# Feed-forward matmuls as lowest-priority filler, half-size attention units in one segment, and LayerNorm scaling shared with a second engine, in a scheduled two-layer kernel

## The chip, the cores and the metric

The kernel runs on one core of one Trainium2 chip. The metric is device time in microseconds (us) of one execution of the whole program. The kernel before was run three times for the first record: 559.99 us median, 558.21 to 562.43. Every experiment below was timed in turn with the kernel before on the same chip.

A core has several engines that each work through their own instruction list in order. The profile calls them PE (TensorE matmuls), PEld (its weight loads, which overlap PE), DVE (VectorE), ACT (ScalarE), POOL (GpSimd) and SP (SyncE, which here issues the DMA transposes).

## The reference

Two equal layers are applied to x of shape 1 x 2048 x 512 in bf16. Cut to what matters:

```python
x = A_x
for layer in (0, 1):
    x = x + A(layernorm(x), wq, wk, wv, wo, beta)   # attention with a memory
    x = x + B(layernorm(x), w1, w3, w2)             # (silu(x@w1) * (x@w3)) @ w2, 512 -> 1376 -> 512

def A(x, ...):                    # 32 heads of 16, four segments of 512 tokens
    M, z = 0, 0
    for s in range(4):
        a_dot = softmax(qs @ ks.T * scale + causal_mask) @ vs
        a_mem = (phi(qs) @ M) / (phi(qs) @ z + 1e-6)       # phi(t) = t+1 if t>0 else exp(t)
        outs.append(g * a_mem + (1 - g) * a_dot)           # g = sigmoid(beta)
        M, z = M + phi(ks).T @ vs, z + sum(phi(ks))        # carried to the next segment
    return concat(outs) @ wo
```

Three dependences matter. A segment needs the memory of the segment before. Layer 1 of a segment needs layer 0's feed-forward result of the same tokens, that is of the same segment. And the value product needs the masked exponentials.

## The kernel before

A Python program builds a list of operations, each with its dependences, buffers, a priority (the smaller number goes first) and an estimated cost. A list scheduler then fixes, before anything runs, the order of every engine's instructions. On the chip each engine follows its list and waits on semaphores. If an estimate is wrong, the order stays as it was, and the engine waits.

Eight attention segments (g = 0 to 7, four in each layer) each go through: LayerNorm (LN), projections q, k, v, the memory read and update, 20 attention units, the output projection, LN again, and the feed-forward network (FFN). The code below is from the kernel; "..." marks cuts.

```python
# cost of one operation on an engine: (engine, time it occupies the engine, time to its result), in ns
def o_act(n, psum=True):
    return ("act", 114.0 + 0.833 * n, (190.0 if psum else 225.0) + 0.833 * n)
def o_dve(n, psum=False, mode=1.0):
    c = n / 0.96 / mode
    return ("dve", c + (75.0 if psum else 45.0), c + (150.0 if psum else 65.0))
def o_pool(n, per=1.04):
    return ("pool", 170.0 + per * n, 170.0 + per * n)
...
mkpool("S", 1)        # one logit buffer of four PSUM banks
mkpool("B", 4)        # four single banks for everything else
e_r = ring("e", 6, [P, 4, 512])       # six buffers of exponentials
xf_r = ring("xf", 1, [P, NCG, 512])   # one buffer of normalised FFN input
...
# the scale 0.5 of the tanh form of silu is put into w2, on POOL
for a in range(2):
    pool(lambda e, a=a: e.tensor_scalar(w2_sb[:, 5 * a:5 * a + 5, :], w2_sb[:, 5 * a:5 * a + 5, :], 0.5, None, op0=ALU.mult),
         2560, ..., prio=0.9)
...
# LayerNorm: after bn_stats, bn_aggr (DVE) and the power -1/2 (POOL), 128 tokens at a time
dve(lambda e, ...: e.tensor_scalar(xn_r[xn.slot][:], x_tok[:, tt, :], mean, rstd,
        op0=ALU.subtract, op1=ALU.mult), 512, mode=1.3, ..., prio=prio, name="norm")
dmaT(...)                                         # transposed by a DMA
...
# attention unit: logits on PE, exp on ACT, causal mask of the 128 diagonal columns on POOL
u = pe(lg, N / 2.4 + 20, mode="R", ...)           # HP priority: first of all
act(... e.activation(e_r[...][:, :, 0:N], S4[:, :, 0:N], ACT.Exp, scale=SCALE), 4 * N, ...)
pool(... e.affine_select(e_r[...][:, :, c:c + 128], ...), 512, ..., name="mask")
...
pe(av, 1280 / 2.4 + 40, mode="C", reads=[... masked exponentials ...], ...)   # value product, after 3 or 5 units
...
# priorities of PE's other work, by segment g
#   projections        g - 0.95 + 0.05 * n        memory matmuls   g + 0.1 to g + 0.42
#   output projection  g + 0.9                    FFN              from g + 1.35 on
```

PE executes in order. If a value product stands at the head of PE's list and its mask is late, all matmuls behind it wait.

The softmax here doesn't subtract the row's maximum and nothing guards it: scores larger than these inputs give would overflow.

## Time and profile before

| | before |
|---|---|
| time, median of 3 | 559.99 us |
| profiled execution | 560.7 us span |
| PE / DVE / ACT / POOL busy | 86% / 79% / 71% / 42% |

The page's first two parts give each engine's busy time over the span, and the span in 40 slices of 14 us. A digit is the busy share of a slice in tenths; in the PEclk row it is the granted clock of the TensorE.

```profile
PE 484.8 (86%) x3836; PEld 198.4 (35%) x3904; DVE 445.5 (79%) x893; ACT 395.5 (71%) x324; POOL 235.2 (42%) x326
...
PE   1837568758999899999989999999999999989897
...
PEclk9956789877999899999999999999999999999999
```

PE is nearly full from slice 11 on. In the first ten slices it has holes, and its clock is low there. Some PE records are missing (3836 matmuls against 3904 weight loads), so PE's busy time before is a little understated.

The groups of instructions give line, engine, operation, tiles and shapes, count, busy us and mean ns, and then the idle time of the engine before them with what ended it.

```profile
L682 ACT ACTIVATE e<-psall 128x2048 bf16<-128x2048 f32 x160 | 300.3, 1877 | 57.5 <-PE psall L674 55.1
...
L700 PE MATMUL psall<-e,va 128*32 128x512 bf16 (+3 forms) x1024 | 49.2, 316 | 6.2 <-POOL e L685 5.4
...
L515 DVE TENSOR_SCALAR xn<-x_tok,ln 128x512 bf16<-128x512 bf16 x64 | 43.6, 713 | 12.2 <-POOL ln L509 7.6
```

The 160 exps set the beat: 1.877 us each. The 64 LN scalings on DVE take 713 ns on average. The busy time by stage, cut at the first exp, the first exps of segments 1 and 2, and the last exp, comes from the windows view. Its columns are the stretch and its length, then busy us (and instructions) of PE, PEld, DVE, ACT and POOL, the granted clock, the DMA share and GB/s.

```profile
20.50:95.00 74.50, 46.81 (x392) 18.04 (x397) 63.10 (x111) 47.00 (x34) 41.84 (x44) 0.75 0.46 125
95.00:153.30 58.30, 44.85 (x389) 16.52 (x394) 43.73 (x96) 47.09 (x37) 26.44 (x37) 0.82 0.31 55
153.30:481.70 328.40, 314.20 (x2670) 128.34 (x2718) 281.01 (x573) 282.61 (x224) 148.97 (x222) 0.99 0.26 50
481.70:560.70 79.00, 70.79 (x358) 32.69 (x363) 50.78 (x92) 13.76 (x24) 4.58 (x6) 1.00 0.17 42
```

Segment 0 (first row) takes 74.5 us, at a granted clock of 0.75. Segments 2 to 7 (third row) take 54.7 us each, with PE almost always busy at full clock. After the last exp comes a tail of 79 us of FFN and output matmuls.

Two causes of segment 0's length can be read directly. First, the chain of waits (start, us, what) shows the memory matmuls behind a DMA transpose:

```profile
30.92 8.29 DMA pkt<-pk
39.21 0.05 issue
39.26 1.09 PE psall L594 x8
40.34 0.57 PE psall L674 x4
```

PE reaches these memory matmuls before their transpose has landed, and the logits behind them (L674) wait too. Second, the timelines of POOL and then of DVE in the same stretch (start, us, engine, operation):

```profile
49.90 6.68 POOL L485 TENSOR_SCALAR w<-w 128x2560 bf16<-128x2560 bf16 x1
...
58.42 6.66 POOL L485 TENSOR_SCALAR w<-w 128x2560 bf16<-128x2560 bf16 x1
```

```profile
50.44 6.93 DVE L515 TENSOR_SCALAR xn<-x_tok,ln 128x512 bf16<-128x512 bf16 x2
57.29 1.27 DVE L441 CAST va<-psall 128x512 bf16<-128x512 f32 x2
58.48 6.74 DVE L515 TENSOR_SCALAR xn<-x_tok,ln 128x512 bf16<-128x512 bf16 x1
```

While POOL scales w2 for 6.7 us, an LN scaling that otherwise takes 0.4 to 0.7 us on DVE lasts as long as POOL's instruction. The evictions queued behind it on DVE wait.

### The profile page before, as it was taken

The page shows a single profiled execution, that of the slowest core. Times are in us where ns is not written, and L with a number is a line of the kernel's source. Part 1 is how long each engine was busy: PE and PEld are TensorE (multiplying, and loading weights), DVE is VectorE, ACT ScalarE, POOL GpSimd, SP SyncE. Part 2 cuts the span into 40 slices and gives each one's busy share as a digit, 9 for nine tenths or more (in the row PEclk, how much of TensorE's full clock was granted, in tenths as well). Part 3 has the DMA queues.
Part 4 walks back from the last instruction along what each step waited for, and adds up shares of the span by engine and source line. Part 5 has one row for each costly group of instructions (what it writes and reads, how often), then busy time and mean ns, then how long its engine had stood idle before and what let it go on. Part 6 is the DMA issues. An engine that isn't in the chain of part 4 may idle for free.

```text
span 560.7 us, 9831 instructions
## 1 busy us (share of the span) xinstructions
PE 484.8 (86%) x3836; PEld 198.4 (35%) x3904; DVE 445.5 (79%) x893; ACT 395.5 (71%) x324; POOL 235.2 (42%) x326
## 2 busy tenths in 40 slices
PE   1837568758999899999989999999999999989897
PEld 0212123222333333333333433443334433434343
DVE  4558999885769787898877989899987897868573
ACT  1736387877987799889878898888998798322130
POOL 7528843453435435545434544444454444210000
PEclk9956789877999899999999999999999999999999
DMA  5793112324211431143223231323113110220301
GB/s 169 243 275 75 39 39 47 49 49 94 39 29 30 67 67 29 29 85 58 47 39 67 49 67 39 67 48 67 39 39 85 48 40 19 67 66 1 76 0 39
DMA packets 106255, 35.31 MB, mean 63 GB/s; under 512 B 100736, under 2 KB 104832, under 8 KB 106208
## 3 DMA queue, kind: packets, MB, share of 16 engines
q1 hardware_dynamic: 102976, 26.76, 24.1%
q0 software_dynamic: 1504, 6.32, 3.2%
q10 hardware_dynamic: 1728, 1.58, 0.9%
q8 instruction: 31, 0.51, 0.4%
q14 instruction: 16, 0.13, 0.1%
HBM read 8.43 MB, written 2.10 MB: 19 GB/s over the span
## 4 chain that ended last, share of the span: by engine, by line
PE 48%; DVE 24%; DMA 11%; issue 7%; ACT 4%; POOL 4%; SPq 1%; POOLq 0%
PE psall L767 19%; PE psall L543 6%; PE psall L791 6%; DMA xg<-xs 5%; PE psall L674 5%; PE psall L700 5%; DVE xn L515 4%; ACT e L682 3%; PE psall L743 3%; PE psall L538 3%; DVE ln L502 2%; DMA ot<-og 2%; DMA pkt<-pk 1%; DVE x_tok L746 1%; DMA xf<-xn 1%
## 5 line engine op out<-in xcount | busy, mean ns | idle before, releaser
L682 ACT ACTIVATE e<-psall 128x2048 bf16<-128x2048 f32 x160 | 300.3, 1877 | 57.5 <-PE psall L674 55.1
L685 POOL TENSOR_SCALAR_AFFINE_SELECT e<-e 128x512 bf16<-128x512 bf16 x256 | 168.3, 675 | 205.7 <-ACT e L682 205.6
L767 PE MATMUL psall<-xf,w 128*128 128x512 bf16 (+1 forms) x678 | 172.5, 386 | 9.8 <-DMA xf<-xn 3.3
L767 PEld LDWEIGHTS psall<-xf,w 128*128 128x128 bf16 (+1 forms) x704 | 65.4, 101 | 90.1 <-issue 18.4
L775 ACT ACTIVATE th<-psall 128x512 bf16<-128x512 f32 (+1 forms) x88 | 52.0, 597 | 54.6 <-PE psall L767 54.5
L791 PE MATMUL psall<-w,h 128*128 128x512 bf16 (+1 forms) x334 | 87.2, 380 | 1.3 <-issue 0.8
L674 PE MATMUL psall<-q,km 32*128 32x512 bf16 (+3 forms) x1024 | 66.1, 313 | 16.0 <-ACT e L682 14.6
L777 DVE SCALAR_TENSOR_TENSOR gp<-th,psall 128x512 bf16<-128x512 bf16 (+1 forms) x88 | 59.1, 678 | 18.0 <-ACT th L775 17.4
L783 DVE TENSOR_TENSOR h<-gp,psall 128x512 bf16<-128x512 bf16 (+1 forms) x88 | 59.4, 678 | 9.2 <-PE psall L767 8.6
L700 PE MATMUL psall<-e,va 128*32 128x512 bf16 (+3 forms) x1024 | 49.2, 316 | 6.2 <-POOL e L685 5.4
L515 DVE TENSOR_SCALAR xn<-x_tok,ln 128x512 bf16<-128x512 bf16 x64 | 43.6, 713 | 12.2 <-POOL ln L509 7.6
L538 PE MATMUL psall<-wv,xa 128*128 128x512 bf16 x123 | 37.4, 418 | 14.6 <-DMA xa<-xn 13.7
L791 PEld LDWEIGHTS psall<-w,h 128*128 128x128 bf16 (+1 forms) x352 | 32.1, 98 | 38.1 <-issue 6.6
L674 PEld LDWEIGHTS psall<-q,km 32*128 32x128 bf16 x1024 | 18.0, 93 | 77.0 <-ACT e L682 66.0
L543 PE MATMUL psall<-xa,wk 128*128 128x512 bf16 x120 | 37.6, 404 | 6.8 <-DVE q L441 5.6
L502 DVE BATCH_NORM_STATS2 ln<-x_tok 128x6 f32<-128x512 bf16 x64 | 42.5, 675 | 0.4
L509 POOL TENSOR_TENSOR ln<-ln,mhalf 128x4 f32<-128x4 f32 (+1 forms) x19 | 18.2, 959 | 46.7 <-DVE ln L507 39.3
L700 PEld LDWEIGHTS psall<-e,va 128*32 128x32 bf16 x1024 | 22.3, 98 | 41.3 <-POOL e L685 21.6
L743 PE MATMUL psall<-wo,ot 128*128 128x512 bf16 x122 | 33.2, 398 | 3.6 <-DMA ot<-og 1.7
L543 PE MATMUL psall<-xa,wq 128*128 128x512 bf16 x123 | 34.2, 382 | 1.8 <-DVE va L441 1.1
L724 POOL TENSOR_TENSOR og<-xg,rd 128x256 bf16<-128x256 bf16 x27 | 20.4, 757 | 28.7 <-DVE rd L718 14.1
L796 DVE TENSOR_TENSOR x_tok<-psall,x_tok 128x512 bf16<-128x512 f32 x32 | 21.9, 684 | 13.2 <-PE psall L791 13.1
(61 smaller groups left out, 437.7 us busy)
## 6 DMA issues: line engine op xcount, KB each, us to landing
w<-in_B_w_dram POOLq DMA_DIRECT2D x2, 1376.0 KB, 11.0
out_dram<-x_tok SPq DMA_DIRECT2D x16, 128.0 KB, 1.8
x_tok<-in_A_x_dram POOLq DMA_DIRECT2D x3, 512.0 KB, 6.1
w<-in_B_w_dram POOLq DMA_DIRECT2D x1, 1280.0 KB, 16.3
xg<-xs SPq DMA_TRANSPOSE x64, 2.4
wq<-in_A_wq_dram ACTq DMA_DIRECT2D x1, 512.0 KB, 4.5
x_tok<-in_A_x_dram SPq DMA_DIRECT2D x4, 128.0 KB, 5.2
wk<-in_A_wk_dram ACTq DMA_DIRECT2D x1, 512.0 KB, 6.8
```

What stands on the lines that cost most here:

```text
L502: dve(lambda e, i=i, tt=tt: e.bn_stats(ln_r[st.slot][:, i, 0:6], x_tok[:, tt, :]), 512, reads=[("x", tt)], writes=[(st, 0, i)], bufs=[st], ...
L515: dve(lambda e, i=i, tt=tt, xn=xn: e.tensor_scalar(xn_r[xn.slot][:], x_tok[:, tt, :], ln_r[st.slot][:, i, 6:7], ln_r[st.slot][:, i, 9:10], ...
L538: fn = lambda e, cg=cg, G=G, B=B, st=st, sp_=sp_: e.matmul(bank(B), xa_r[X.slot][:, cg, 128 * G:128 * G + 128], wv_sb[:, cg, :], start=st, ...
L543: fn = lambda e, cg=cg, G=G, B=B, st=st, sp_=sp_, w=w: e.matmul(bank(B), w[:, cg, 128 * G:128 * G + 128], xa_r[X.slot][:, cg, :], start=st ...
L674: o = e.matmul(S4[:, pg, c:c + n], km_r[z.km.slot][32 * pg:32 * pg + 32, ee, G, 128 * j:128 * j + 128], q_r[z.q.slot][32 * pg:32 * pg + 32 ...
L682: act(lambda e, N=N, ebuf=ebuf: e.activation(e_r[ebuf.slot][:, :, 0:N], S4[:, :, 0:N], ACT.Exp, scale=SCALE), 4 * N, reads=[(sbuf_, 0)], w ...
L685: pool(lambda e, ebuf=ebuf, c=c: e.affine_select(e_r[ebuf.slot][:, :, c:c + 128], e_r[ebuf.slot][:, :, c:c + 128], pattern=[[0, 4], [1, 128]],
L700: o = e.matmul(bank(X)[32 * pg:32 * pg + 32, 128 * j:512], va_r[z.va.slot][:, j, VS * (8 * G + 2 * pg + ee):VS * (8 * G + 2 * pg + ee) + 3 ...
L767: prev = pe(lambda e, cg=cg, ft=ft, fw=fw, B=B, w=w: e.matmul(bank(B)[0:fw, :], w[:, cg, 128 * ft:128 * ft + fw], xf_r[X.slot][:, cg, :], ...
L777: dve(lambda e, fw=fw, B=B, th=th, gp=gp: e.scalar_tensor_tensor(gp_r[gp.slot][0:fw, :], th_r[th.slot][0:fw, :], 1.0, bank(B)[0:fw, :], AL ...
L783: dve(lambda e, fw=fw, B=B, gp=gp, h=hs[ft]: e.tensor_tensor(h_r[h.slot][0:fw, :], gp_r[gp.slot][0:fw, :], bank(B)[0:fw, :], ALU.mult), 51 ...
L791: prev = pe(lambda e, i=i, ft=ft, fw=fw, B=B, h=hs[ft]: e.matmul(bank(B), h_r[h.slot][0:fw, 128 * i:128 * i + 128], w2_sb[0:fw, ft, :], st ...
```

## The change

The intent is to use PE's holes in the early segments better and to relieve DVE. Its core, with cuts marked by "...":

```diff
 # 1. recalibrated cost estimates (o_act, o_dve and the sizes given to some operations)
-    return ("dve", c + (75.0 if psum else 45.0), c + (150.0 if psum else 65.0))
+    return ("dve", c + (60.0 if psum else 30.0), c + (150.0 if psum else 100.0))
 ...
 # 2. the first segment's attention units in halves, in two logit buffers
-    mkpool("S", 1)
+    mkpool("S", 2)
+    SPLIT = (0,)
+                groups = [(0, 1), (2, 3)] if g in SPLIT else [(0, 1, 2, 3)]
+                for pgs in groups:
 ...             # logits and exp for each group: 40 exps of 1024 columns in segment 0
 # 3. LN scaling on DVE or POOL, whichever can start first
-            dve(lambda e, i=i, tt=tt, xn=xn: e.tensor_scalar(
+            S.add([o_dve(512, False, 0.95)] + ([] if fine else [o_pool(512)]), lambda e, i=i, tt=tt, xn=xn: e.tensor_scalar(
 ...
-                bufs=[st, xn], prio=prio, name="norm")
+                bufs=[st, xn], hold=[dst], prio=prio, name="norm")
 # 4. memory add on DVE or POOL
-                dve(lambda e, og=og, om=oms[G]: e.tensor_tensor(fl(og_r, og), ..., ALU.add), 512, mode=1.4,
+                S.add([o_dve(512, False, 1.2), o_pool(512, 2.25)], lambda e, og=og, om=oms[G]: e.tensor_tensor(
 # 5. priorities, and releases by attention progress
+            gate = units.get((g - 1, (3 * n) // 2))
-                ..., prio=p0 + 0.001 * cg,                          # projections
+                ..., prio=p0 + 0.001 * cg - 500, gates=[gate],
-   prio=g + 0.3 (dacc)      prio=g + 0.1 (mden)      prio=g + 0.12 + 0.1 * G (mnum)
+   prio=g + 0.3 - 900       prio=g + 0.1 - 800       prio=g + 0.12 + 0.1 * G - 800
-            pr = g + 0.25 * G                                       # scaling of the attention output
+            pr = g - 1 + 0.25 * G
-   prio=g + 0.9 + 0.001 * i                                         # output projection
+   prio=g + 0.9 + 0.001 * i - 900
-            X = layer_norm(s, "xa", g - 1.0, gates=[first_unit.get(g - 2)], fine=(g == 0))
+            X = layer_norm(s, "xa", g - 1.0, gates=[units.get((g - 2, 10))], fine=(g == 0))
-            X2 = layer_norm(s, "xf", g + 1.1)
+            X2 = layer_norm(s, "xf", g + 0.1)
```

The FFN's own priority is not touched. It becomes the lowest because the rest of PE's work is raised above it. "oadd" is the memory add, "dacc" the memory update, "mden" and "mnum" the memory read.

## The prediction

> **What bounds it now.** The page: PE busy 86%, DVE 79%, ACT 71%; median 560 us. Cutting the trace at the exps (160 of 1.877 us, by the groups): start 20.5 us, segments' attention 74.5, 58.3, then about 54.7 each; the last exp ends at 481.7; then a 79 us tail in which PE works off 341 feed-forward (FFN) and output matmuls. At 0.216 us a full matmul (dense stretches on the chain of waits) PE has about 444 us of work: 49 of 54.7 us in segments 2 to 7, but only 34.5 of 74.5 in segment 0 and 36.5 of 58.3 in segment 1. So 60 us of slack lie in the first two segments; later PE (90%) and ACT (48 us per segment) are both nearly full, and FFN moved there only changes places.
>
> Segment 0's chain shows why: memory-accumulate matmuls queued ahead of logits wait for a transpose of pk (8.3 us; ACT idles 7.9); two LN scalings on DVE take 6.7 us each, exactly while POOL scales w2; each exp waits about 0.7 us for the next logits (one logit buffer), at a granted clock of 0.7 to 0.8.
>
> **What the change does**, from the instruction order:
> - Memory accumulation and next-segment projections leave most of segment 0 (PE work 34.5 to 26.0 us). The 8 us stall should go. ACT work there falls 48.5 to 44.7 us.
> - Segment 0's 20 exps become 40 of 1024 columns in two buffers. From the exp's cost and the 597 ns of a 512-column eviction I estimate 1.02 us each: 3.4 us more ACT work, against about 12 us of handoff waits removed.
> - 34 of 64 LN scalings and 11 of 24 memory adds go to POOL. POOL scaled 512 columns in 1.51 us, DVE takes 0.41 (median), the scheduler assumes 0.70: POOL rises from 235 to about 300 us, DVE loses about 20. "SBUF — State Buffer" of the Trainium skill (section "SBUF: two separate sides") says DVE and GpSimd share an exclusively locked port pair; the 6.7 us scalings agree. So part of DVE's gain returns as lock waits; DVE is no limit after segment 1, so a few us either way.
> - FFN slides back: in the last quarter segment PE's backlog grows by some 63 matmuls, and the tail by 63 x 0.216 = 14 us.
> - Layer 1's projections need layer 0's FFN; lowest priority delays them: segment 7's are squeezed into its own first quarter. I expect an exp gap of several us there, filled with FFN.
>
> **Sum.** Start 20.5; segment 0: 55 (-20); segment 1: 55 (-3); segments 2 to 7: 326 (-2: lighter FFN, but ACT allows little and the layer-1 gap costs); tail 94 (+15). Total 551 us, 80% range 537 to 564. Moved FFN itself is neutral: what counts is PE's idle time. Chances: faster by over 2% 0.42, within 2% 0.53, slower 0.05.
>
> **What would show it.** Segment 0: first to 20th exp takes 50 to 60 us, no ACT wait over 4 us behind a pk transpose. Filler: last exp near 455 us, tail near 94 us at over 90% PE. POOL: busy near 300 us, scaling near 1.5 us each, DVE 415 to 435. Layer debt: longest late exp gap near the segment 6/7 boundary.
>
> **What would make it wrong.** If w2's scaling still blocks DVE with projections or evictions behind it, segment 0 stays above 62 us and the gain vanishes. If POOL's slow scalings delay masks or the LN chain, segments 4 to 7 lengthen. If the recalibrated costs make the static order fit better, segments 2 to 7 fall below 52 us each and the time drops under 540.

## The result, and the profile after

The changed kernel is slower: 597.14 us median of four runs (594.80 to 599.66), against 560.87 us of the four runs of the kernel before in the same rounds. The ratio is 1.0653, with a 95% interval of 1.0582 to 1.0723. Ratios here and below are the mean time of one kernel's fast runs over that of the other's of the same rounds, so not quite the ratio of the medians quoted.

Cut at the same places (the exps' start times in the trace), the time went here:

| us | start | seg 0 | seg 1 | segs 2 to 7 | tail |
|---|---|---|---|---|---|
| before | 20.5 | 74.5 | 58.3 | 328.4 | 79.0 |
| predicted | 20.5 | 55 | 55 | 326 | 94 |
| after | 20.7 | 61.7 | 63.8 | 361.5 | 89.6 |
| after less predicted | 0 | +7 | +9 | +35 | -4 |

The page of the changed kernel:

```profile
PE 522.8 (88%) x3904; PEld 202.9 (34%) x3904; DVE 433.4 (73%) x850; ACT 394.6 (66%) x340; POOL 316.9 (53%) x373
...
PE   2957788697997999989898898889989889999997
...
PEclk9959766887998999989898988979999799999999
```

PE's share is no lower than before (88% against 86%, which the missing records understate a little), yet the kernel is slower. The PEclk row shows why that is no contradiction: in the middle and late slices, where before had almost only nines, there are now eights and sevens. A matmul at a lower clock is busy for longer. So PE's busy share is not PE's useful work.

The chain's shares by engine, first before and then after (a q marks an engine's sequencer; "issue" is time in which the engine waited for nothing that the profile shows):

```profile
PE 48%; DVE 24%; DMA 11%; issue 7%; ACT 4%; POOL 4%; SPq 1%; POOLq 0%
```

```profile
PE 55%; DVE 20%; POOL 15%; ACT 6%; DMA 2%; issue 1%; SPq 0%; ACTq 0%; POOLq 0%
```

DMA left the chain: the wait for the transpose of pk in segment 0 is gone, as intended. POOL entered it, with 15%. The groups say with what:

```profile
L690 ACT ACTIVATE e<-psall 128x2048 bf16<-128x2048 f32 (+1 forms) x180 | 301.5, 1695 | 90.2 <-PE psall L682 88.8
...
L710 PE MATMUL psall<-e,va 128*32 128x512 bf16 (+3 forms) x1024 | 53.8, 337 | 32.3 <-POOL e L695 30.3
...
L515 POOL TENSOR_SCALAR xn<-x_tok,ln 128x512 bf16<-128x512 bf16 x34 | 72.3, 2133 | 0.5
```

An LN scaling of 512 columns takes 2133 ns on POOL. The scheduler's estimate for it was 170 + 1.04 x 512 = 702 ns. PE's waits for masks before value products rose from 5.4 to 30.3 us. In the first group the two exp sizes are mixed; kept apart, the half-size one is

```profile
L690 ACT ACTIVATE e<-psall 128x1024 bf16<-128x1024 f32 x40 | 38.6, 1055 | 16.9 <-PE psall L682 16.9
```

The windows, in the same columns as before:

```profile
20.70:82.40 61.70, 46.87 (x330) 13.83 (x329) 49.38 (x83) 41.71 (x44) 47.11 (x44) 0.76 0.51 136
82.40:146.20 63.80, 51.00 (x433) 19.09 (x432) 54.13 (x111) 48.10 (x36) 37.60 (x46) 0.77 0.32 63
146.20:507.70 361.50, 330.50 (x2703) 128.00 (x2703) 267.71 (x542) 280.17 (x221) 197.81 (x251) 0.94 0.23 47
507.70:597.30 89.60, 86.01 (x411) 39.09 (x408) 55.25 (x92) 19.50 (x34) 20.77 (x13) 1.00 0.14 33
```

In segments 2 to 7 PE issues slightly fewer weight loads than before (2703 against 2718), but is idle for 31.0 us (361.5 less 330.5), 19.5 us of it ended by POOL's masks (2.2 us before), and the mean granted clock is 0.94 instead of 0.99. POOL's load there rose from 149.0 to 197.8 us.

How one slow scaling becomes a PE wait is seen in a timeline of POOL and of PE at the same moment:

```profile
255.29 4.33 POOL L515 TENSOR_SCALAR xn<-x_tok,ln 128x512 bf16<-128x512 bf16 x2
259.57 1.82 POOL L695 TENSOR_SCALAR_AFFINE_SELECT e<-e 128x512 bf16<-128x512 bf16 x3
```

```profile
257.81 1.04 PE L801 MATMUL psall<-w,h 96*128 96x512 bf16 x4
260.86 1.08 PE L710 MATMUL psall<-e,va 128*32 128x512 bf16 x16 [2.01 <-POOL e L695]
```

Two scalings hold POOL for 4.3 us. Three masks queue behind them. The scheduler had put value products on PE where it thought the masks would be done, so PE stands for 2.01 us (in brackets: idle time before, and what ended it). The 16 value matmuls then take 1.08 us; the same 16 take 0.73 us where the clock stays full.

The granted clock often falls to a half near such waits. In segments 2 to 7 of the changed kernel PE has eight idle gaps over 1.5 us (1.9 to 2.7 us), and every one is ended by a POOL mask. Around six of them, from 0.8 us before their end to 1.7 us after it, a stretch at half clock begins. In all, nine half-clock stretches of 3.4 or 6.8 us begin in these segments, 41.0 us together; the other three have no single gap over 1.5 us near them. The kernel before has one, of 3.4 us.

The kept traces show what the single gaps don't. The clock changes only on a grid of 3.41 us. Cut along this grid, all nine half-clock stretches follow a grid step in which PE was busy for only 29 to 64% of the time; of the other steps at full clock just two were busy for less than 65% (49 and 63%). So in these traces it is the idle time added up over a grid step that goes with the drop, whoever caused it (one exception: in e4 below a step of 47%, with a gap of 3.1 us, was not followed by a drop). In e9 below, which has no LN scaling on POOL and no PE gap over 1.5 us in these segments, six such stretches (24 us) follow steps of 40 to 62%. An estimate from the changed kernel's stretches: if PE was needed throughout, 41.0 us at half rate lose at most 20 us of work.

One more line of the story is the layer debt that the prediction named. The chain before segment 7 (start, us, what):

```profile
430.96 0.70 DVE x_tok L806
...
433.19 1.03 POOL ln L509
...
434.83 1.48 POOL xn L515
...
436.88 2.10 POOL xn L515
...
440.31 0.73 PE psall L710 x16
441.04 1.83 PE psall L539 x8
```

Layer 0's last FFN addition for this segment ends at 431.7 us; LN runs after it, part of it through POOL's slow scalings, and segment 7's value projections (L539) start at 441.0 us. The longest time from one late exp to the next is here: 15.7 us. (Here and below such times run from the start of one exp to the start of the next, so each contains one exp, 1.9 us at full size; ACT waits for the other 13.9 us.)

### The profile page after: what moved, and what is told of

Read it like the earlier page. It is cut to its first block, busy times and chain, and to the rows that moved or that the text cites. A ratio compares the mean times of both kernels' runs of the same rounds, so it can differ in the third digit from the quotient of the medians.

```text
span 597.3 us, 9915 instructions
## 1 busy us (share of the span) xinstructions
PE 522.8 (88%) x3904; PEld 202.9 (34%) x3904; DVE 433.4 (73%) x850; ACT 394.6 (66%) x340; POOL 316.9 (53%) x373
## 3 DMA queue, kind: packets, MB, share of 16 engines
q1 hardware_dynamic: 102976, 26.76, 22.4%
## 4 chain that ended last, share of the span: by engine, by line
PE 55%; DVE 20%; POOL 15%; ACT 6%; DMA 2%; issue 1%; SPq 0%; ACTq 0%; POOLq 0%
PE psall L777 17%; PE psall L801 11%; POOL xn L515 7%; PE psall L710 6%; PE psall L544 6%; PE psall L682 6%; ACT e L690 5%; PE psall L753 4%; POOL e L695 4%; PE psall L539 4%; DVE ln L502 2%; DVE km L559 2%; DVE px L573 2%; POOL ln L509 2%; DVE k L441 2%; DMA xa<-xn 1%
## 5 line engine op out<-in xcount | busy, mean ns | idle before, releaser
L690 ACT ACTIVATE e<-psall 128x2048 bf16<-128x2048 f32 (+1 forms) x180 | 301.5, 1695 | 90.2 <-PE psall L682 88.8
L695 POOL TENSOR_SCALAR_AFFINE_SELECT e<-e 128x512 bf16<-128x512 bf16 x256 | 165.6, 667 | 180.5 <-ACT e L690 180.3
L777 PEld LDWEIGHTS psall<-xf,w 128*128 128x128 bf16 (+1 forms) x704 | 66.6, 101 | 85.5 <-issue 14.4
L785 ACT ACTIVATE th<-psall 128x512 bf16<-128x512 f32 (+1 forms) x88 | 51.8, 599 | 61.7 <-PE psall L777 61.7
L682 PE MATMUL psall<-q,km 32*128 32x512 bf16 (+3 forms) x1024 | 77.0, 327 | 8.9 <-ACT e L690 8.7
L710 PE MATMUL psall<-e,va 128*32 128x512 bf16 (+3 forms) x1024 | 53.8, 337 | 32.3 <-POOL e L695 30.3
L515 POOL TENSOR_SCALAR xn<-x_tok,ln 128x512 bf16<-128x512 bf16 x34 | 72.3, 2133 | 0.5
L793 DVE TENSOR_TENSOR h<-gp,psall 128x512 bf16<-128x512 bf16 (+1 forms) x88 | 59.4, 679 | 13.9 <-PE psall L777 13.5
L539 PE MATMUL psall<-wv,xa 128*128 128x512 bf16 x128 | 40.4, 448 | 14.7 <-DMA xa<-xn 14.7
L441 DVE CAST xs<-psall 128x512 bf16<-128x512 f32 x43 | 29.4, 684 | 27.6 <-PE psall L710 27.5
L710 PEld LDWEIGHTS psall<-e,va 128*32 128x32 bf16 x1024 | 23.3, 102 | 74.2 <-POOL e L695 44.3
L682 PEld LDWEIGHTS psall<-q,km 32*128 32x128 bf16 x1024 | 20.1, 94 | 81.7 <-ACT e L690 59.9
L801 PEld LDWEIGHTS psall<-w,h 128*128 128x128 bf16 (+1 forms) x352 | 32.5, 100 | 43.0 <-issue 11.4
L544 PE MATMUL psall<-xa,wq 128*128 128x512 bf16 x128 | 39.1, 411 | 1.0 <-DMA xa<-xn 1.0
```

What stands on the lines that cost most here:

```text
L515: S.add([o_dve(512, False, 0.95)] + ([] if fine else [o_pool(512)]), lambda e, i=i, tt=tt, xn=xn: e.tensor_scalar(xn_r[xn.slot][:], x_tok[ ...
L539: fn = lambda e, cg=cg, G=G, B=B, st=st, sp_=sp_: e.matmul(bank(B), xa_r[X.slot][:, cg, 128 * G:128 * G + 128], wv_sb[:, cg, :], start=st, ...
L544: fn = lambda e, cg=cg, G=G, B=B, st=st, sp_=sp_, w=w: e.matmul(bank(B), w[:, cg, 128 * G:128 * G + 128], xa_r[X.slot][:, cg, :], start=st ...
L682: o = e.matmul(S4[:, sps(pg), c:c + n], km_r[z.km.slot][32 * pg:32 * pg + 32, ee, G, 128 * j:128 * j + 128], q_r[z.q.slot][32 * pg:32 * pg ...
L690: act(lambda e, N=N, ebuf=ebuf, pgs=pgs, sps=sps: e.activation(e_r[ebuf.slot][:, pgs[0]:pgs[-1] + 1, 0:N], S4[:, sps(pgs[0]):sps(pgs[-1]) ...
L695: pool(lambda e, ebuf=ebuf, c=c: e.affine_select(e_r[ebuf.slot][:, :, c:c + 128], e_r[ebuf.slot][:, :, c:c + 128], pattern=[[0, 4], [1, 128]],
```

## The experiments

Two theories stood at the start. Theory A: POOL's slow LN scalings delay the causal masks, so value products and with them all of PE wait, and the clock drops. Its main rival, B: the new priorities and releases put PE's work in a worse order, so exps wait for projections and PE for its evictions, whatever POOL does. The parts of the change were then put back and tried alone until the sum closed. All 18 kernels gave results that the comparison with the reference accepted. In the results below, "before" is the median of the kernel before in the same rounds. The edits are shortened; where one line holds both signs, the part after - became the part after +. Not every range was hit: e1 to e4 came out between the ranges of the two theories (e3 0.8 us above one of them), because both hold; e12 was far above its range, e7, e8, e15 and e17 lay above every range that was expected, and e18 lay below.

### First round: what of the change costs the time (before: 561.3 us)

**e1_short_pool.** The changed kernel with its instruction order unaltered, but POOL's LN scalings on 128 of their 512 columns. Its output is wrong, which doesn't matter for the time. Three quarters of such a tile keep stale normalised values, which the tolerance of the comparison did not notice.

```diff
+    def NC(e):
+        return 128 if e is nc.gpsimd else 512
-                xn_r[xn.slot][:], x_tok[:, tt, :], ...
+                xn_r[xn.slot][:, 0:NC(e)], x_tok[:, tt, 0:NC(e)], ...
```

> The changed kernel with every engine's order unchanged, but the 34 LN scalings that POOL does cover 128 of 512 columns (wrong result on purpose), so each should take about 0.6 to 0.7 us, as the scheduler had priced it, and not 2.13. Theory A (POOL's slow scalings sit in front of the causal masks, and PE waits in order for the masks): 545 to 560 us, PE's waits on POOL for the value matmuls fall from about 75 us to under 30 us. Theory B (the new priorities: feed-forward last, layer 1 waiting for it): 585 us or more, segment 6 still near 70 us.

Measured: 572.95 us, ratio 1.0203 (1.0153 to 1.0252). The run's profile, groups and then the window of segments 2 to 7:

```profile
L518 POOL TENSOR_SCALAR xn<-x_tok,ln 128x128 bf16<-128x128 bf16 x34 | 29.9, 885 | 2.1 <-DMA xf<-xn 1.5
```

```profile
L713 PE MATMUL psall<-e,va 128*32 128x512 bf16 (+3 forms) x1024 | 50.8, 322 | 13.9 <-POOL e L698 10.6 <-DVE gp L790 0.9 <-DVE h L796 0.9
```

```profile
140.30:480.80 340.50, 320.83 (x2703) 126.56 (x2704) 269.28 (x544) 280.10 (x221) 175.63 (x252) 0.97 0.25 50
```

With the same order on every engine, 34 shorter POOL instructions took 24 us off the time (597.14 to 572.95). PE's waits for masks fell from 30.3 to 10.6 us, PE's idle time in segments 2 to 7 from 31.0 to 19.7 us (340.5 less 320.83), and the clock rose from 0.94 to 0.97. So POOL's slow scalings cost about two thirds of the loss of 36 us, but not all of it: A alone had expected 545 to 560 us. By itself the run doesn't separate the masks from other paths that a shorter scaling also shortens. The trace speaks for the masks: PE's waits for them account for 19.7 us, while DVE's busy time hardly moved (433.4 to 432.3 us), so it is not a lock on DVE; what the LN chain contributes stays open. (The expectation's 75 us adds the waits of the weight loads; so counted, 74.6 us fell to 40.5 and not below 30.) Between the two profiled executions, 27.0 us apart, PE's idle time fell by 12.2 us and its busy time, for the same 3904 matmuls in the same order, by 14.8 us: about half of the gain came as shorter matmuls. From 885 ns at 128 columns and 2133 ns at 512 the cost of this operation on POOL is about 3.25 ns a column, plus about 0.47 us.

**e2_norm_dve.** The changed kernel with LN scaling on DVE only (the memory add may still go to POOL), scheduled anew.

```diff
-            S.add([o_dve(512, False, 0.95)] + ([] if fine else [o_pool(512)]), lambda ...
+            S.add([o_dve(512, False, 0.95)], lambda ...
```

> The changed kernel with LN scaling on DVE only; the memory add may still go to POOL; the scheduler lays out a new order. A: 545 to 562 us, POOL busy about 245 us. B: 585 us or more.

Measured: 573.42 us, ratio 1.0212 (1.0158 to 1.0266). This is the size of e1's gain by another way. A new large hole showed: 22.4 us from one exp to the next just before segment 7.

**e3_norm_priced.** The changed kernel with POOL's price for the scaling set to 2.13 us, as measured.

```diff
-            ... + ([] if fine else [o_pool(512)]), lambda ...
+            ... + ([] if fine else [o_pool(512, 3.83)]), lambda ...
```

> The changed kernel, in which the scheduler prices POOL's LN scaling at the measured 2.13 us in place of 0.70; POOL still does 24 of them. If A's harm is mainly that the static order was laid for 0.70 us, this recovers most: 550 to 570 us. If the POOL time itself is the harm wherever it stands, it recovers about 10 of 34: 580 to 590. B: 590 or more.

Measured: 570.83 us, ratio 1.0175 (1.0116 to 1.0234). Even at the right price 24 of the 64 scalings went to POOL (34 in the changed kernel). The scheduler takes the engine that can *start* first and does not compare when the engines would finish; so a price alone cannot keep a slow operation off an idle engine. It does let the rest of the order be planned for the true duration, and that is enough: PE's waits for masks (L710) fell to 6.0 us, though each scaling on POOL took 2.18 us.

```profile
L710 PE MATMUL psall<-e,va 128*32 128x512 bf16 (+3 forms) x1024 | 51.8, 328 | 15.7 <-POOL e L695 6.0 <-DVE om L641 4.7 <-DVE h L793 2.9
```

With 24 slow scalings left on POOL, e3 is no slower than e2 with none (the intervals overlap). And e8 below loses 20 us with only 22 scalings on POOL, priced at 0.70 us. So the harm was mainly an order laid for 0.70 us, more than the 2.13 us in themselves (that e3 also has ten scalings fewer on POOL was not tested apart).

**e4_prio_back.** The changed kernel with all priorities and releases of the kernel before, POOL sharing kept (29 scalings go to POOL).

```diff
-   projections  p0 + 0.001*cg - 500, gates=[gate]     +   p0 + 0.001*cg
-   dacc g+0.3-900, mden g+0.1-800, mnum ...-800       +   g+0.3, g+0.1, g+0.12+0.1*G
-   output projection g+0.9-900                        +   g+0.9
-   attention scaling g-1+0.25*G, LN xf g+0.1          +   g+0.25*G, g+1.1
-   LN xa gate: unit 10 of segment g-2                 +   unit 0
```

> The changed kernel with all PE priorities, the release of projections and the LN priorities as in the kernel before; POOL sharing, half-size units and new costs stay (29 LN scalings on POOL). A: 580 us or more, since POOL still holds the masks. B: 550 to 565.

Measured: 568.97 us, ratio 1.0144 (1.0083 to 1.0204). So B is right too: the priorities carry a loss of their own, of like size. PE's waits for masks are still there:

```profile
L710 PE MATMUL psall<-e,va 128*32 128x512 bf16 (+3 forms) x1024 | 50.2, 320 | 27.5 <-POOL e L695 25.1 <-DVE rm L623 1.3 <-DVE gp L787 0.9
```

### Second round: the parts alone (before: 562.46 us)

**e5_dve_prio_back.** The changed kernel with LN scaling and memory add on DVE only, and priorities and releases as before. What remains of the change are the half-size units, the recalibrated costs and the hold of the LN's destination.

```diff
 # the edits of e2 and e4 together, and
-                S.add([o_dve(512, False, 1.2), o_pool(512, 2.25)], lambda e, og=og, om=oms[G]: e.tensor_tensor(
+                S.add([o_dve(512, False, 1.2)], lambda e, og=og, om=oms[G]: e.tensor_tensor(
```

> The changed kernel with LN scaling and memory add on DVE alone and all priorities as before: what stays are half-size units in segment 0, two logit slots and the new costs. If the 12 us that the change still loses without slow POOL scalings come from the priorities (layer 1 waiting for late feed-forward): 545 to 558 us. If they come from the new costs or the half-size units: 565 to 575.

Measured: 548.41 us, ratio 0.9776 (0.9721 to 0.9831): faster than before. The windows of segment 0 and of segments 2 to 7:

```profile
20.80:84.70 63.90, 48.10 (x325) 14.10 (x326) 51.87 (x86) 41.77 (x45) 41.33 (x42) 0.71 0.50 132
142.00:469.30 327.30, 321.88 (x2756) 129.79 (x2755) 283.51 (x577) 281.06 (x224) 155.76 (x233) 1.00 0.25 51
```

Segments 2 to 7 take 327.3 us (close to the 326 predicted, but by luck: this kernel lacks the moved FFN from which the prediction had its number), with PE idle for only 5.4 us (327.3 less 321.88) at full clock. Both losses are gone together. Segment 0 still takes 63.9 us, at a clock of 0.71.

**e6_before_split.** The kernel before with only part 2 of the change, the half-size units.

```diff
-    mkpool("S", 1)
+    mkpool("S", 2)
+    groups = [(0, 1), (2, 3)] if g in SPLIT else [(0, 1, 2, 3)]     # SPLIT = (0,), as in the change
```

> The kernel before with half-size logit units in segment 0 alone. If the exp's wait for its one logit buffer costs time there, as I predicted: 548 to 556 us. If segment 0 is held by evictions and transposes anyway: 557 to 565.

Measured: 553.81 us, ratio 0.9852 (0.9793 to 0.9911). Segment 0 went from 74.5 to 65.0 us. This part gains 8 to 9 us alone.

**e7_before_prio.** The kernel before with only part 5, priorities and releases.

```diff
 # all edits of part 5 of the change, on the kernel before; without hold=[dst] of the LN scaling
```

> The kernel before with the new priorities and releases alone. If feed-forward last is harmful by itself (late layer-0 feed-forward holds layer 1's projections, an exp gap over 8 us before segment 7): 565 to 580. If it is neutral or good: 545 to 560, since the memory stall of 8 us in segment 0 goes.

Measured: 586.59 us, ratio 1.0461 (1.0408 to 1.0513). The number overstates what the priorities cost in the change. The trace shows LN scalings for the FFN taking the buffers of normalised rows while they wait for the single FFN input buffer, so that segment 6's projections start at 389.8 us, after the previous FFN's up matmuls end at 380.0 us; 22.8 us pass from one exp to the next there. The changed kernel's hold (hold=[dst]) is there to avoid this. So this is not a clean copy of the part, and e9 replaces it.

**e8_before_pool_norm.** The kernel before with only part 3 and its hold, LN scaling on DVE or POOL (22 of 64 go to POOL).

```diff
-            dve(lambda e, i=i, tt=tt, xn=xn: e.tensor_scalar(
+            S.add([o_dve(512, False, 1.3)] + ([] if fine else [o_pool(512)]), lambda e, i=i, tt=tt, xn=xn: e.tensor_scalar(
-                bufs=[st, xn], prio=prio, name="norm")
+                bufs=[st, xn], hold=[dst], prio=prio, name="norm")
```

> The kernel before with POOL allowed to do LN scalings alone (22 of 64 go there). If slow scalings ahead of masks cost by themselves, in proportion to 24 us for 34: about 15 us more, 570 to 580, with more half-clock stretches after segment 1. If they cost only together with the new priorities: 557 to 566.

Measured: 581.62 us, ratio 1.0362 (1.0313 to 1.0411), a loss of about 20 us. The 22 scalings took 2186 ns each, and PE's waits for masks rose from 5.4 to 21.8 us:

```profile
L700 PE MATMUL psall<-e,va 128*32 128x512 bf16 (+3 forms) x1024 | 49.5, 317 | 23.6 <-POOL e L685 21.8 <-DVE q L441 1.0 <-DVE va L441 0.5
```

Part 3 alone slows the kernel, in an order that has nothing else of the change. Its hold is not to blame: e5 has it too and is faster than before.

### Third round: the priorities, and the w2 scaling (before: 561.7 us)

**e9_dve_new_prio.** The changed kernel with LN scaling and memory add on DVE only, and the new priorities.

```diff
 # against the changed kernel: o_pool taken out of both S.add option lists
```

> The changed kernel with LN scaling and memory add on DVE alone, new priorities kept. It differs from e5_dve_prio_back by the priorities only, and from e2_norm_dve by the memory add on POOL only. If the priorities cost: 566 to 576 us with an exp gap over 12 us before segment 7. If the memory add on POOL was the cost in e2: 546 to 556.

Measured: 567.61 us, ratio 1.0111 (1.0054 to 1.0168). With e4, e5 and the change itself this fills a two-by-two table:

| ratio to before | all on DVE | shared with POOL |
|---|---|---|
| priorities as before | 0.9776 (e5) | 1.0144 (e4) |
| new priorities | 1.0111 (e9) | 1.0653 (the change) |

Sharing costs 3.7% of the time before at the old priorities and 5.4% at the new ones; the priorities cost 3.4% without sharing and 5.1% with it. They add up, and seem to make each other somewhat worse (each ratio is known to about 0.6%). PE's waits for masks are 1.9 us in e5 and 4.8 us in e9, against 25.1 and 30.3 us where POOL shares. In e9 the largest hole lies before segment 7: 24.3 us from one exp to the next. Layer 0's last down matmuls for it end at 411.5 us, its projections begin at 419.2 and its logits at 433.1; PE is busy with other FFN matmuls for most of that time.

**e10_ffn0_raised.** That hole suggested a cause: layer 0's FFN, now lowest, is late for layer 1. So e9 with the layer-0 FFN raised by 500.

```diff
-        base, step = g + 1.35, 1.0 / 132
+        base, step = g + 1.35 - (500 if g < 4 else 0), 1.0 / 132
```

> As e9, but layer 0's feed-forward is raised to the level of the projections (base priority lower by 500 for segments 0 to 3); layer 1's stays last. If what costs in e9 is layer 0's feed-forward delaying layer 1's projections: 545 to 556 us, gap before segment 7 under 6 us. If feed-forward as filler costs anyhow: 563 or more.

Measured: 576.18 us, ratio 1.0259 (1.0202 to 1.0315): slower than e9. The hole before segment 7 went, but others came up in several segments (10.4, 8.7 and 7.0 us from one exp to the next). So the theory that a late layer-0 FFN is the one cause falls.

**e11_no_w2_scale.** e5 without POOL's scaling of w2. The factor 0.5 is put into the FFN's residual add, which DVE does anyway.

```diff
-        pool(... e.tensor_scalar(w2_sb[...], w2_sb[...], 0.5, None, op0=ALU.mult) ...)      # all three
-            dve(lambda e, tt=tt, B=B: e.tensor_tensor(x_tok[:, tt, :], bank(B), x_tok[:, tt, :], ALU.add), 512, True,
+            dve(lambda e, tt=tt, B=B: e.scalar_tensor_tensor(x_tok[:, tt, :], bank(B), 0.5, x_tok[:, tt, :], ALU.mult, ALU.add), 512, True,
```

> As e5_dve_prio_back (548 us), without POOL's scaling of w2 by 0.5; the factor goes into the residual add. If POOL's two 6.7 us scalings hold DVE and with it segment 0 (63.8 us in e5): segment 0 falls to 53 to 58 us and the total to 538 to 545. If the stalls there are transposes behind the weight loads: under 3 us gained.

Measured: 538.48 us, ratio 0.9579 (0.9524 to 0.9633). This is the fastest kernel of the study. The window of segment 0:

```profile
20.70:69.00 48.30, 38.63 (x316) 12.18 (x322) 37.24 (x82) 39.87 (x44) 25.96 (x39) 0.86 0.65 175
```

Segment 0 fell from 63.9 to 48.3 us. DVE's busy time there fell from 51.9 to 37.2 us and POOL's by 15.4 us; the three scalings had taken 15.0 us in e5. The residual adds cost the same as before (680 ns against 686 ns). Not all of it was kept: segments 2 to 7 took 334.4 us instead of e5's 327.3, so that the whole gained 10 us and not 15.6.

**e12_both.** e10 with the edit of e11.

```diff
 # the edits of e10 and of e11 on e9
```

> e10 and e11 together: if both causes are right and add up, 534 to 548 us, the best of all; if the two do not add, within 2 us of the better one.

Measured: 573.58 us, ratio 1.0214 (1.0162 to 1.0266). Segment 0 took 45.2 us, but e10's holes remain. The hope for 534 to 548 us was missed: most of what segment 0 gave was lost later.

### Fourth and fifth rounds: which of the priorities (before: 562.72 and 561.89 us)

Each of these starts from e5 (ratio 0.9776), except e14.

**e13_gates_only.** e5 with the releases by attention progress, without raised priorities.

```diff
-   prio=p0 + 0.001 * cg,                                  +   prio=p0 + 0.001 * cg, gates=[gate],
-   X = layer_norm(..., gates=[units.get((g - 2, 0))])     +   gates=[units.get((g - 2, 10))]
```

> e5_dve_prio_back (548 us) plus only the release of projections by attention progress (and of the LN before them). If the releases are the costly part of the priorities (the 19 us between e9 and e5): 560 to 570. If not: 545 to 552.

Measured: 548.01 us, ratio 0.9751 (0.9723 to 0.9780). The releases neither cost nor gain anything that shows.

**e14_no_gates.** e9 without the releases, the raised priorities kept.

```diff
-   prio=p0 + 0.001 * cg - 500, gates=[gate],              +   prio=p0 + 0.001 * cg - 500,
-   X = layer_norm(..., gates=[units.get((g - 2, 10))])    +   gates=[units.get((g - 2, 0))]
```

> e9_dve_new_prio (568 us) without those releases: projections free as soon as their input is there, feed-forward still last. If the releases are the costly part: 546 to 556. If feed-forward last is: 563 to 573, with the long exp gap before segment 7.

Measured: 567.03 us, ratio 1.0096 (1.0059 to 1.0133), as e9. The hole before segment 7 (22.4 us) is there without the releases too. Both runs acquit the releases.

**e15_mem_out_first.** e5 with memory matmuls, output projection, LN for the FFN and attention scaling raised as in the change, but not the projections.

```diff
+   dacc g+0.3-900, mden g+0.1-800, mnum ...-800, output projection g+0.9-900
+   attention scaling g-1+0.25*G, LN xf g+0.1
```

> e5_dve_prio_back plus only the raised priorities of memory matmuls, output projection and the LN and scaling around them; projections stay as in e5, so layer 1's projections still rank with feed-forward. If feed-forward behind the projections is the cost: 545 to 553. If raising memory and output work is: 560 to 570.

Measured: 582.41 us, ratio 1.0358 (1.0326 to 1.0390).

**e16_add_pool.** e5 with the memory add allowed on POOL (16 of 24 go there, 1219 ns each).

```diff
-                S.add([o_dve(512, False, 1.2)], lambda ...
+                S.add([o_dve(512, False, 1.2), o_pool(512, 2.25)], lambda ...
```

> e5_dve_prio_back plus only the memory add shared with POOL (1.15 us there against 0.42 on DVE). If it costs as e2 against e9 suggests: 551 to 556. If it is neutral: 546 to 550.

Measured: 549.57 us, ratio 0.9771 (0.9738 to 0.9803). At the old priorities sharing this addition is neutral, so there part 3 is what makes sharing costly. At the new ones it may not be quite neutral: e2, which differs from e9 by it alone, has 1.0212 against 1.0111, though in other rounds.

**e17_pe_part.** Of e15 only PE's part: memory matmuls and output projection raised.

```diff
+   dacc g+0.3-900, mden g+0.1-800, mnum ...-800, output projection g+0.9-900
```

> e5_dve_prio_back (548 us) plus only the raised PE priorities of memory matmuls and output projection. If e15's loss (582 us) lies in PE's order: 573 to 586. If it lies in DVE's order (the LN before the feed-forward and the output scaling raised): 545 to 553.

Measured: 587.92 us, ratio 1.0468 (1.0436 to 1.0500). This part alone costs about 39 us against e5 (0.0692 x 561.89). The loss lies in the late segments:

```profile
143.90:511.00 367.10, 335.95 (x2757) 130.47 (x2758) 286.12 (x576) 286.59 (x233) 154.04 (x230) 0.98 0.23 46
```

Segments 2 to 7 take 367.1 us instead of e5's 327.3, with the same number of matmuls and PE idle for 31 us instead of 5. ACT's timeline at the sixth unit of segment 5:

```profile
323.90 1.88 ACT L690 ACTIVATE e<-psall 128x2048 bf16<-128x2048 f32 x1 [1.29 <-PE psall L682]
328.89 0.60 ACT L440 ACTIVATE va<-psall 128x512 bf16<-128x512 f32 x1 [3.12 <-PE psall L539]
...
334.42 1.88 ACT L690 ACTIVATE e<-psall 128x2048 bf16<-128x2048 f32 x1 [0.34 <-PE psall L710]
```

After 323.9 us the next exp comes 10.5 us later. Between them ACT evicts value projections (va) that PE has only just computed. The trace's matmul starts agree: segment 5's logits start at 309.7 us but its first value product at 333.6, while in e5 they are 8.6 us apart (301.6 and 310.2). The units run ahead until the six buffers of exponentials are full; they can only be emptied by value products, which need the late projections. The same happens at the sixth unit of segments 6 and 7 (9.0 and 8.9 us); the first exps of these segments come late too, 10.7 and 11.4 us after the exp before.

**e18_dve_part.** Of e15 only DVE's part: LN for the FFN and attention scaling raised.

```diff
-            pr = g + 0.25 * G                      +            pr = g - 1 + 0.25 * G
-            X2 = layer_norm(s, "xf", g + 1.1)      +            X2 = layer_norm(s, "xf", g + 0.1)
```

> e5_dve_prio_back plus only the raised priorities of the LN before the feed-forward and of the output scaling. PE's order to blame: 545 to 553. DVE's order to blame: 565 to 586.

Measured: 542.29 us, ratio 0.9656 (0.9622 to 0.9691): about 7 us better than e5. So raising DVE's part is a gain, and the harm of e15 is all in PE's part.

## Why the prediction was wrong

The range was 537 to 564 us and the result 597 us. The sum of steps, each the difference of two ratios times 562 us:

| step | kernels | us |
|---|---|---|
| half-size units in segment 0 | before to e6 | -8 |
| recalibrated costs, hold, the rest | e6 to e5 | -4 |
| new priorities and releases | e5 to e9 | +19 |
| LN scaling and memory add shared with POOL | e9 to the change | +30 |
| sum | before to the change | +37 |

The second line is not resolved: the intervals of e5 and e6 overlap.

**The step that failed first: "part of DVE's gain returns as lock waits; DVE is no limit after segment 1, so a few us either way".** The prediction looked for POOL's cost on DVE and on average load, and took 1.51 us a scaling from POOL's scaling of 512 columns of w2. That is another form, with one constant; the LN scaling takes two per-partition operands and measured 2.133 us. More important, the load is not where it hurts. POOL is busy for 53% of the span, and its total of 316.9 us was within 6% of the predicted 300. But POOL works in order, and the masks stand behind the scalings. PE's value products wait for those masks, and PE also works in order. The cost is therefore latency times the places where PE meets it, and then the granted clock. e1 shows it in the same instruction order: 24 us for shorter POOL operations alone. e8 shows it on the kernel before: 20 us for 22 scalings. The prediction had this as its second warning ("If POOL's slow scalings delay masks or the LN chain, segments 4 to 7 lengthen"), and they did: 249.8 us together instead of 218.5 before, by the starts of the exps. Not all of that is POOL's: they take 233.4 us with short scalings in the same order (e1), 242.9 without sharing (e9), and 228.6 with sharing alone (e8). Yet it gave slower by over 2% a chance of 0.05. It knew that POOL's true duration was more than twice the scheduler's 0.70 us, and did not ask which waits in a static order that difference would turn into; e3, with the right price, shows that it was mainly this difference that cost.

**The second failed step: "Moved FFN itself is neutral", with segments 2 to 7 at 326 us.** The new priorities cost 19 us by themselves (e5 to e9). It is not the releases (e13, e14), and not the raised DVE work (e18 gains). Raising PE's memory matmuls and output projection costs most: 39 us alone (e17), with value projections late and exp buffers full. Raising the projections as well wins part of that back (e9 and e14 against e15, where 1.0358 becomes 1.0111 and 1.0096). What is left then shows most in the layer debt. The prediction foresaw its place and named an exp gap "of several us"; ACT's wait there was 13.9 us in the changed kernel and 22.4 in e9. Raising the layer-0 FFN closed that gap but opened others, and gained nothing (e10).

**The size of segment 0's term.** 55 us were predicted, 61.7 measured. The prediction's first warning gives most of the reason: w2's scaling still blocks DVE. In e5, which has the same half-size units, taking that scaling away brings segment 0 from 63.9 to 48.3 us (e11). The warning put the limit at 62 us, and the result lies just there, but the effect was treated as a risk and not priced in the sum. Sharing adds to it: without it segment 0 took 57.4 us (e9), with w2's scaling still in place.

**What was right.** The wait for the transpose of pk is gone, and DMA's share of the chain fell from 11% to 2%. The half-size exp took 1.055 us against the estimate of 1.02, and halving the units gains by itself (e6). The tail took 89.6 us with PE busy 96% of it, against 94 us at over 90% (but it began at 507.7 us and not near 455). DVE's busy time of 433.4 us lies in the range of 415 to 435. The layer debt sits where it was expected.

**A cost that was not in the sum at all: the clock.** In segments 2 to 7 the mean granted clock was 0.99 before, 0.94 after, 0.97 in e1 and e9, and 1.00 in e5. The Trainium skill, page "TensorE: Matmul & The Clock Gate", section "HAM oscillation — how this bites in real kernels", gives "no PE-idle gaps >~3.4µs" as the rule. In these segments of the changed kernel no gap was longer than 2.7 us, and still nine half-clock stretches came, each after a grid step of 3.41 us in which PE was busy for 29 to 64%. The measurement decides: shorter gaps than the page's went with a lower clock here, and three of the stretches came without any gap over 1.5 us. No experiment isolates the clock's share from the wait's; the estimate of at most 20 us above bounds the clock's share in these segments, whatever made the clock fall.

**The shared port pair.** The prediction cited the page "SBUF — State Buffer", section "SBUF: two separate sides", for an exclusive lock between DVE and GpSimd (POOL). By that section the lock concerns DVE instructions in a two-port mode or with two SBUF inputs. The trace agrees: DVE scalings of 6.7 us beside POOL's w2 scalings of 6.7 us, and segment 0 shorter by 15.6 us when those are removed. In the changed kernel, while POOL scales w2 from 48.67 to 55.37 us, DVE's statistics and PSUM evictions keep their usual 0.6 to 0.7 us, and a tensor_scalar that starts at 51.37 us is held until 55.65. The prediction drew the right fact from it and named the w2 scaling among its warnings, but priced only the new scalings and not the old w2 scaling, where the effect was large.

**What stays open.** Why raised memory and output matmuls push the value projections so late is not shown step by step; e17 shows that they do. That early memory-read matmuls hold the four single PSUM banks while DVE works through its reciprocals is a guess that no run tests. Projections raised alone above the FFN, and e11 with DVE's part of e18, were not run; by their separate gains the latter should be faster still, but parts of this change did not always add up.

## What to carry to other kernels

Before work is moved to an idle-looking engine, take the duration of the same operation in the same form on that engine, give it to the scheduler (here the right price alone won back 26 us, e3), and ask which short, urgent operations will stand behind it in that engine's order; the cost is their latency on the busiest engine, not the idle engine's load. In a statically ordered kernel, test the parts of a scheduling change one by one: here half-size units, raised DVE priorities and a scaling folded into a later addition gain 8, 7 and 10 us, and were hidden behind two parts that lost 30 and 19. A busy share of PE that holds or rises is no gain if the granted clock fell: read the two rows together.

## What the Trainium skill lacked or had wrong

- "GPSIMD Engine Reference", section "3.1 Elementwise — side-by-side cycle accounting", states a best case of about 1.8 cycles an element (769 ns for 512 elements) and about 2.6 for a two-input tensor_tensor. It has no figure for a tensor_scalar with two per-partition operands. Here 512 bf16 columns took 2133 ns and 128 took 885 ns, so about 3.25 ns a column; a two-input addition of 512 bf16 columns took 1153 ns in the changed kernel.
- "TensorE: Matmul & The Clock Gate", section "HAM oscillation — how this bites in real kernels": the rule of no idle gaps over about 3.4 us is too lenient for this kernel. Around six of eight PE waits of 1.9 to 2.7 us the granted clock fell to a half, for 3.4 or 6.8 us; two such waits (2.1 and 2.3 us) had no such stretch, and three stretches came without a single gap over 1.5 us. What all nine stretches had before them was a grid step of 3.41 us with PE busy for 29 to 64%. The page's next section ("A second HAM failure mode: psum-queue depth-cycling") does tell of short idles that make the clock swing, but gives no such figure.
- "SBUF — State Buffer", section "SBUF: two separate sides": nothing wrong. A DVE instruction of 0.4 to 0.7 us that met a POOL instruction of 6.7 us took 6.7 us, as an exclusive lock would have it.
